# Loading w2 and w_out first, and forming their product while the other inputs arrive

## The chip, the cores and the metric

The kernel runs on one core of a Trainium2 chip. The metric is the device time of one execution in microseconds (us). Each time below is the median of several executions; the kernel before was run again on the same chip, in the same rounds, beside every experiment. A ratio is the mean time of one kernel's fast runs over that of the kernel before in the same rounds, with a 95% interval, so it isn't quite the ratio of the medians quoted. Profiles are of one execution each. A time "at 45.6" is counted from the start of that profile's span.

## The reference, cut to what matters

```python
k_proj = einsum('ks,bhsd->bhkd', E, k)          # 8 batches, 8 heads, 1024 tokens, 64 dims, 64 projected keys
v_proj = einsum('ks,bhsd->bhkd', F, v)
attn   = softmax(q @ k_proj.T / 8)
x      = attn @ v_proj                          # as 8192 tokens x 512
g      = maximum(x @ w1, x @ w2)                # w1, w2: 512 x 1024
out    = g @ w_out                              # w_out: 1024 x 512
```

The kernel uses maximum(h1, h2) = relu(h1 - h2) + h2. With wd = w1 - w2 and M = w2 @ w_out,

    out = relu(x @ wd) @ w_out + x @ M

so x goes through one wide product less, and M has to be formed once. Both products of later units are done with seven block products in place of eight, which takes sums and differences of blocks: those of w_out and M are called T, those of wd are t_w, those of g and x are "sums".

## The kernel before

All inputs are float32 in HBM and are cast to float16 on the way by DMAs issued from GpSimd. Batch 0's loads come first, then w2 and w1 in four pieces each, then w_out whole:

```python
for h0 in (0, H // 2):
    for n, src in (("k", k), ("q", q)):
        for h in (h0, h0 + H // 4):
            load(tiles[0], n, src, 0, h, h + H // 4)     # 256 KB of float16 each
    ...
load(tiles[0], "v", v, 0, 0, H // 2)
load(tiles[0], "v", v, 0, H // 2, H)
...
for f0 in range(0, DF, 256):
    for w_sb, w in ((w2_sb, moe_w2), (w1_sb, moe_w1)):
        nc.gpsimd.dma_start(out=w_sb[:, :, f0 : f0 + 256], in_=...)
nc.gpsimd.dma_start(out=wo_sb, in_=...)
```

Then come fillers, meant to keep TensorE's clock up (`warm(n)`: n matmuls of 128x512 whose result nobody reads), batch 0's attention, and its 16 up products (x @ wd), called slots. M is formed after the last of them, its transposes of w2 lying among them:

```python
def step_w2t(f0):                   # 8 transposes of w2, one copy on ScalarE
    ...
def step_m(r):                      # 8 matmuls of 128x512, one copy on ScalarE
    m_ps = mm_bank()
    for fb in range(NFB):
        nc.tensor.matmul(out=m_ps, lhsT=w2t_sb[:, fb, r * 128 : (r + 1) * 128],
                         rhs=wo_sb[:, fb, :], start=(fb == 0), stop=(fb == NFB - 1))
    nc.scalar.copy(out=m_sb[:, r, :], in_=m_ps)

slots = [ ... (2, u1[0]), (3, u1[1]), (4, u0[2]), (None, wt[0]), (5, u0[3]), ...
    *((16 + n, lambda n=n: step_m(n)) for n in range(NDC)) ]
for key, s_, *a in ( ...
    (15, sums_g, U[0, 0], (0, 1)), (16, step_t, 0), (16, sums_g, U[0, 0], (2, 3)),
    *((17 + i // 3, step_tw, i) for i in range(4)), (19, open_box, 3)):
    at_slot((0, key), s_, *a)       # VectorE's work beside slots 15 to 19
```

Batch 1's projection, its attention and the first down products follow ("batch 1's attention" below), then a steady pipeline to the end.

The softmax here doesn't subtract the row's maximum and nothing guards it: scores larger than these inputs give would overflow.

## Time and profile before

| | |
|---|---|
| time | 336.87 us (336.1 to 337.24, 3 runs) |
| span of the profiled run | 335.3 us |
| busy: PE, VectorE (DVE), ScalarE (ACT) | 325.3, 243.2, 225.3 us |
| DMA landings: first k, q pieces; v; w2 and w1; w_out | 8.2 to 17.3; 22.4; 23.7 to 33.1; 38.1 us |
| first projection of k / up products without a gap / M / batch 1's projection / batch 2's | 9.7 / 28.5 / 43.4 / 50.2 / 70.4 us |

In a timeline line the first two numbers are the start and the duration in us, then come engine, source line, operation, output<-inputs, shape and count, and in brackets how long the engine had idled and what ended it. The last row of the table is what the study follows: after batch 2's projection both kernels do the same, so its start tells the outcome.

### The profile page before, as it was taken

How to read it: one execution, taken by the hardware profiler on the slowest of the kernel's cores; microseconds unless marked ns; L12 is line 12 of the kernel's file. 1: busy time of each engine (PE TensorE's matmuls, PEld its weight loads, DVE VectorE, ACT ScalarE, POOL GpSimd, SP SyncE). 2: the span in 40 equal slices, each digit the busy share in tenths (PEclk: the TensorE clock that was granted, in tenths of full speed). 3: DMA queues.
4: the chain of work that ended last, by engine and by line, in shares of the span. 5: the costliest groups of instructions: out<-in, count | busy, mean ns of one | idle time of the engine just before them, and what ended most of it. 6: DMA issues, size and time to landing. Idle time of an engine off the chain costs nothing.

```text
span 335.3 us, 7334 instructions
## 1 busy us (share of the span) xinstructions
PE 325.3 (97%) x3020; PEld 245.9 (73%) x3020; DVE 243.2 (73%) x430; ACT 225.3 (67%) x354; POOL 34.4 (10%) x51
## 2 busy tenths in 40 slices
PE   6998999999999999999999999999999999999994
PEld 3544547578767887788878887888788888888883
DVE  1246898987776968787877967796878787868572
ACT  1287332955879787678778887878777877654541
POOL 7544002020003000200003000300000000000000
PEclk9799999999999999999999999999999999999998
DMA  7999999999886996699897999699742120202132
GB/s 136 204 201 199 207 207 207 218 232 187 174 190 82 208 226 158 118 178 243 184 164 110 225 179 200 113 211 231 183 95 94 33 97 31 96 31 96 34 125 94
DMA packets 71474, 51.98 MB, mean 155 GB/s; under 512 B 25233, under 2 KB 71313, under 8 KB 71441
## 3 DMA queue, kind: packets, MB, share of 16 engines
q0 software_dynamic: 30336, 28.31, 53.3%
q1 hardware_dynamic: 41104, 23.21, 27.7%
q8 instruction: 23, 0.38, 0.4%
q14 instruction: 11, 0.08, 0.1%
HBM read 57.15 MB, written 16.78 MB: 220 GB/s over the span
## 4 chain that ended last, share of the span: by engine, by line
PE 84%; DVE 8%; ACT 2%; DMA 2%; issue 1%; SPq 0%; DVEq 0%
PE mm_ps L699 39%; PE mm_ps L621 24%; PE mm_ps L467 4%; PE att_ps L180 3%; PE att_ps L365 3%; PE mm_ps L503 2%; PE mm_ps L280 2%; DMA big<-in_F_dram 2%; PE mm_ps L180 2%; DVE qt_sb L241 2%; PE mm_ps L139 1%; DVE xt_sb L446 1%; DVE o_sb L723 1%; DVE gt_sb L636 1%; DVE big L582 1%
## 5 line engine op out<-in xcount | busy, mean ns | idle before, releaser
L592 ACT COPY p_sb<-mm_ps 128x512 f32<-128x512 f32 x172 | 97.8, 597 | 38.0 <-PE mm_ps L621 23.5
L699 PEld LDWEIGHTS <-big 128*128 128x128 f16 x768 | 73.3, 98 | 14.6 <-issue 6.2
L699 PE MATMUL mm_ps<-T_sb,big 128*128 128x256 f16 x576 | 77.4, 273 | 0.0
L636 DVE TENSOR_TENSOR gt_sb<-mm_ps,p_sb 128x512 f16<-128x512 f32 x56 | 38.6, 689 | 48.4 <-PE mm_ps L621 26.7
L621 PE MATMUL mm_ps<-big,big 128*128 128x256 f16 x336 | 50.4, 272 | 0.2 <-DVE gt_sb L636 0.2
L621 PEld LDWEIGHTS <-big 128*128 128x128 f16 x448 | 43.8, 98 | 6.2 <-issue 0.4
L699 PEld LDWEIGHTS <-gt_sb 128*128 128x128 f16 x384 | 35.6, 98 | 12.3 <-issue 8.1
L699 PE MATMUL mm_ps<-wo_sb,gt_sb 128*128 128x256 f16 x256 | 42.7, 273 | 0.1
L621 PEld LDWEIGHTS <-wd_sb 128*128 128x128 f16 x336 | 32.9, 98 | 3.8
L621 PE MATMUL mm_ps<-xt_sb,wd_sb 128*128 128x256 f16 x224 | 33.6, 273 | 0.0
L381 DVE TENSOR_TENSOR xt_sb<-att_ps,ld_sb 128x1024 f16<-128x1024 f32 x24 | 29.3, 1222 | 1.8 <-ACT ld_sb L377 1.7
L723 DVE TENSOR_TENSOR o_sb<-mm_ps,p_sb 128x512 f32<-128x512 f32 x32 | 21.9, 685 | 9.4 <-PE mm_ps L699 5.9
L299 ACT ACTIVATE ex_sb<-mm_ps 128x512 f16<-128x512 f32 x40 | 21.8, 597 | 7.1 <-PE mm_ps L280 7.0
L377 ACT ACTIVATE ld_sb<-ld_sb 128x1024 f32<-128x1024 f32 x24 | 26.4, 1099 | 0.1
L374 ACT ACTIVATE ld_sb<-att_ps 128x1024 f32<-128x1024 f32 x24 | 24.8, 1035 | 0.6 <-PE att_ps L365 0.6
L699 PE MATMUL mm_ps<-m_sb,xt_sb 128*128 128x256 f16 x128 | 24.4, 273 | 0.0
L639 DVE TENSOR_SCALAR gt_sb<-gt_sb 128x512 f16<-128x512 f16 (+1 forms) x56 | 21.0, 374 | 1.9
L671 ACT ACTIVATE gt_sb<-mm_ps 128x512 f16<-128x512 f32 x28 | 16.8, 601 | 8.1 <-PE mm_ps L621 8.1
L582 DVE TENSOR_TENSOR big<-gt_sb 128x1024 f16<-128x1024 f16 x32 | 21.9, 685 | 0.3
L699 PE MATMUL mm_ps<-T_sb,gt_sb 128*128 128x256 f16 x128 | 21.5, 273 | 0.0
L699 PE MATMUL mm_ps<-wo_sb,big 128*128 128x256 f16 x128 | 21.5, 273 | 0.0
L699 PEld LDWEIGHTS <-xt_sb 128*128 128x128 f16 x192 | 18.8, 98 | 2.2
(106 smaller groups left out, 438.1 us busy)
## 6 DMA issues: line engine op xcount, KB each, us to landing
out_dram<-o_sb SPq DMA_DIRECT2D x63, 256.0 KB, 2.5
k_sb<-in_k_dram POOLq DMA_DIRECT2D x7, 1024.0 KB, 10.3
v_sb<-in_v_dram POOLq DMA_DIRECT2D x7, 1024.0 KB, 16.4
q_sb<-in_q_dram POOLq DMA_DIRECT2D x7, 1024.0 KB, 21.7
big<-in_moe_w_dram POOLq DMA_DIRECT2D x8, 256.0 KB, 12.6
k_sb<-in_k_dram POOLq DMA_DIRECT2D x4, 256.0 KB, 8.1
q_sb<-in_q_dram POOLq DMA_DIRECT2D x4, 256.0 KB, 9.2
v_sb<-in_v_dram POOLq DMA_DIRECT2D x2, 512.0 KB, 11.9
```

The source lines that it names most:

```text
L299: nc.scalar.activation(out=t["ex"][p][:, e, :], in_=banks[e], func=ACTF.Exp, scale=scale)
L374: nc.scalar.activation(out=ld, in_=dn_ps, func=ACTF.Ln)
L377: nc.scalar.activation(out=ld, in_=ld, func=ACTF.Exp, scale=-1.0)
L381: nc.vector.tensor_tensor(out=t["xt"][:, p, :, :], in0=at_ps, in1=ld, op=ALU.mult)
L582: nc.vector.tensor_tensor(out=S(i), in0=x, in1=y, op=op)
L592: copy(out=x, in_=bank)
L621: nc.tensor.matmul(out=bank[:, m * W : (m + 1) * W], lhsT=w_[:, n_, (2 * d + m) * 128 : (2 * d + m + 1) * 128], rhs=a[:, n_, :], start=(n ...
L636: nc.vector.tensor_tensor(out=c_blk(j, c), in0=two(x), in1=two(y), op=ALU.add)
L639: nc.vector.tensor_scalar_max(ap, ap, 0.0)
L671: nc.scalar.activation(out=out, in_=in_, func=ACTF.Relu)
L699: nc.tensor.matmul(out=bank[:, i * CH : (i + 1) * CH], lhsT=a(c)[:, i * 128 : (i + 1) * 128], rhs=w_(c), start=(n is not None and m == (lo ...
L723: nc.vector.tensor_tensor(out=o_sb, in0=two(x), in1=two(y), op=ALU.add)
```

## The change

The intent: PE waits for its first data until 9.7 us anyway. If w2 and w_out come first, M can be formed then, piece by piece as they land, and 8.7 us of PE work leave the middle.

```diff
+    for f0 in range(0, DF, 256):
+        fb = f0 // 128
+        load_w(w2_sb, moe_w2, f0, f0 + 256)
+        nc.gpsimd.dma_start(out=wo_sb[:, fb : fb + 2, :], in_=...[:, fb : fb + 2, :])
+        if f0 == 0:
+            make_identity(nc, ident)
     for h0 in (0, H // 2):
         ... loads of k and q ...
     load(tiles[0], "v", v, 0, 0, H // 2)
     load(tiles[0], "v", v, 0, H // 2, H)
     for f0 in range(0, DF, 256):
-        ... w2 and w1 ...
-    nc.gpsimd.dma_start(out=wo_sb, ...)
+        load_w(w1_sb, moe_w1, f0, f0 + 256)
     ...
+    m_ps = [mm_bank() for _ in range(NDC)]
+    def step_m(f0):                          # 8 matmuls: this piece's part of all four banks
+        for fb in (f0 // 128, f0 // 128 + 1):
+            for r in range(NDC):
+                nc.tensor.matmul(out=m_ps[r], lhsT=w2t_sb[:, fb, r * 128 : (r + 1) * 128],
+                    rhs=wo_sb[:, fb, :], start=(fb == 0), stop=(fb == NFB - 1), ...)
+    ... 6 fillers ...
+    step_w2t(0); step_m(0); step_w2t(256); step_eft(0); step_eft(1); step_m(256)
+    step_w2t(512); step_m(512); step_w2t(768); step_m(768)
+    for r in range(NDC):
+        eng = nc.vector.tensor_copy if r % 2 else nc.scalar.copy
+        eng(out=m_sb[:, r, :], in_=m_ps[r])
 ... batch 0's attention ...
+    step_t(0)                                # ahead of step_kv(t, 0, 4, "k")
     ...
+    step_t(1)                                # ahead of step_wd(0)
 ... up products: the four step_w2t taken out, slots 16 to 19 now empty ...
-        (15, sums_g, ...), (16, step_t, 0), (16, sums_g, ...), *((17 + i // 3, step_tw, i) ...),
+        (15, sums_g, ...), (15, sums_g, ...),
 ... batch 1's attention ...
-        if n in (1, 5):
-            at_slot(key, step_t, 1, (0, 1) if n == 1 else (2, 3))
+        if n in (2, 4, 7, 10):
+            at_slot(key, step_tw, (2, 4, 7, 10).index(n))
```

(The statements joined by semicolons are on lines of their own in the file, and `step_w2t`'s copy is halved between ScalarE and VectorE.)

More of the change, by code (lines that the diff above doesn't have):

```diff
@@ L109, with load_w @@
         alloc(tiles[0], n)
+    w1_sb = big(1).rearrange("p (r f) -> p r f", r=NDC)
+    w2_sb = big(2).rearrange("p (r f) -> p r f", r=NDC)
+    w2t_sb = big(3).rearrange("p (f m) -> p f m", f=NFB)
+    wo_sb = const.tile([128, NFB, DM], FP16)
+    def load_w(w_sb, w, f0, f1):
+        nc.gpsimd.dma_start(
+            out=w_sb[:, :, f0:f1], in_=w[:, f0:f1].rearrange("(r p) f -> p r f", p=128)
+        )
+    for f0 in range(0, DF, 256):
+        fb = f0 // 128
+        load_w(w2_sb, moe_w2, f0, f0 + 256)
+        nc.gpsimd.dma_start(
+            out=wo_sb[:, fb : fb + 2, :],
+            in_=moe_w_out.rearrange("(r p) f -> p r f", p=128)[:, fb : fb + 2, :],
+        )
+        if f0 == 0:
+            ident = const.tile([128, 128], FP32)
+            make_identity(nc, ident)
     for h0 in (0, H // 2):
@@ L113 @@
                 load(tiles[0], n, src, 0, h, h + H // 4)
-        if h0 == 0:
-            ident = const.tile([128, 128], FP32)
-            make_identity(nc, ident)
     load(tiles[0], "v", v, 0, 0, H // 2)
     load(tiles[0], "v", v, 0, H // 2, H)
-    w1_sb = big(1).rearrange("p (r f) -> p r f", r=NDC)
-    w2_sb = big(2).rearrange("p (r f) -> p r f", r=NDC)
-    wo_sb = const.tile([128, NFB, DM], FP16)
     for f0 in range(0, DF, 256):
-        for w_sb, w in ((w2_sb, moe_w2), (w1_sb, moe_w1)):
-            nc.gpsimd.dma_start(
-                out=w_sb[:, :, f0 : f0 + 256],
-                in_=w[:, f0 : f0 + 256].rearrange("(r p) f -> p r f", p=128),
-            )
-    nc.gpsimd.dma_start(out=wo_sb, in_=moe_w_out.rearrange("(r p) f -> p r f", p=128))
+        load_w(w1_sb, moe_w1, f0, f0 + 256)
     ones16 = const.tile([128, 512], FP16)
@@ L141, in warm, with step_eft @@
             )
-    warm(8)
     ident16 = const.tile([128, 128], FP16)
     nc.vector.tensor_copy(out=ident16, in_=ident)
+    m_sb = const.tile([128, NDC, DM], FP16)
     eft = const.tile([128, 2, NC, KP], FP16)
     ef_v = ef_sb.rearrange("kp i (p c) -> kp i c p", c=NC)
-    for i in range(2):
-        eft_ps = mm_bank()
+    def step_eft(i):
+        eft_ps = att_banks()[:, 0, :]
         for c in range(NC):
@@ L157, with step_w2t @@
             )
-        warm(2)
-        eng = nc.scalar.copy if i else nc.vector.tensor_copy
-        eng(out=eft[:, i, :, :].rearrange("p c k -> p (c k)"), in_=eft_ps)
+        nc.vector.tensor_copy(out=eft[:, i, :, :].rearrange("p c k -> p (c k)"), in_=eft_ps)
+    def step_w2t(f0):
+        ps_t = att_banks(FP16)[:, 0, :]
+        for f in range(2):
+            for r in range(NDC):
+                nc.tensor.transpose(
+                    out=ps_t[:, (f * NDC + r) * 128 : (f * NDC + r + 1) * 128],
+                    in_=w2_sb[:, r, f0 + f * 128 : f0 + (f + 1) * 128],
+                    identity=ident16,
+                )
+        for f, eng in enumerate((nc.scalar.copy, nc.vector.tensor_copy)):
+            eng(out=w2t_sb[:, f0 // 128 + f, :], in_=ps_t[:, f * DM : (f + 1) * DM])
+    m_ps = [mm_bank() for _ in range(NDC)]
+    def step_m(f0):
+        for fb in (f0 // 128, f0 // 128 + 1):
+            for r in range(NDC):
+                nc.tensor.matmul(
+                    out=m_ps[r], lhsT=w2t_sb[:, fb, r * 128 : (r + 1) * 128],
+                    rhs=wo_sb[:, fb, :],
+                    start=(fb == 0), stop=(fb == NFB - 1), skip_group_check=True,
+                )
+    w_ps = att_banks()[:, 0, :]
+    for _ in range(6):
+        nc.tensor.matmul(out=w_ps, lhsT=ones16[:, 0:128], rhs=ones16, start=True, stop=True)
+    step_w2t(0)
+    step_m(0)
+    step_w2t(256)
+    step_eft(0)
+    step_eft(1)
+    step_m(256)
+    step_w2t(512)
+    step_m(512)
+    step_w2t(768)
+    step_m(768)
+    for r in range(NDC):
+        eng = nc.vector.tensor_copy if r % 2 else nc.scalar.copy
+        eng(out=m_sb[:, r, :], in_=m_ps[r])
     def new_attn(t):
@@ L456 @@
     wd_sb = const.tile([128, NDC, DF], FP16)
-    m_sb = const.tile([128, NDC, DM], FP16)
-    w2t_sb = big(3).rearrange("p (f m) -> p f m", f=NFB)
     def up_slots(t, j):
@@ L484, in step_wd @@
         )
-    def step_w2t(f0):
-        ps_t = mm_bank(FP16)
-        for f in range(2):
-            for r in range(NDC):
-                nc.tensor.transpose(
-                    out=ps_t[:, (f * NDC + r) * 128 : (f * NDC + r + 1) * 128],
-                    in_=w2_sb[:, r, f0 + f * 128 : f0 + (f + 1) * 128],
-                    identity=ident16,
-                )
-        fb = f0 // 128
-        nc.scalar.copy(
-            out=w2t_sb[:, fb : fb + 2, :].rearrange("q f m -> q (f m)"), in_=ps_t
-        )
-    def step_m(r):
-        m_ps = mm_bank()
-        for fb in range(NFB):
-            nc.tensor.matmul(
-                out=m_ps, lhsT=w2t_sb[:, fb, r * 128 : (r + 1) * 128], rhs=wo_sb[:, fb, :],
-                start=(fb == 0), stop=(fb == NFB - 1),
-            )
-        nc.scalar.copy(out=m_sb[:, r, :], in_=m_ps)
     NG = NFB // 2
@@ L819 @@
     u0, u1 = [*up_slots(t, 0)], [*up_slots(t, 1)]
-    wt = [lambda f0=f0: step_w2t(f0) for f0 in range(0, DF, 256)]
     wd = [lambda f0=f0: step_wd(f0) for f0 in range(0, DF, 256)]
@@ L831 @@
         (0, u0[0]), (None, f(two_at, 1, 1)), (1, u0[1]), (None, lambda: loads(1, "v", "q", "k")),
-        (None, wd[1]), (2, u1[0]), (3, u1[1]), (4, u0[2]), (None, wt[0]), (5, u0[3]),
-        (None, wd[2]), (None, wt[1]), (6, u1[2]), (7, u1[3]), (8, u0[4]), (9, u0[5]), (None, wd[3]),
-        (None, wt[2]), (10, u1[4]), (11, u1[5]), (12, u0[6]), (13, u0[7]), (None, wt[3]),
+        (None, wd[1]), (2, u1[0]), (3, u1[1]), (4, u0[2]), (5, u0[3]),
+        (None, wd[2]), (6, u1[2]), (7, u1[3]), (8, u0[4]), (9, u0[5]), (None, wd[3]),
+        (10, u1[4]), (11, u1[5]), (12, u0[6]), (13, u0[7]),
         (14, u1[6]), (15, u1[7]),
-        *((16 + n, lambda n=n: step_m(n)) for n in range(NDC)),
+        *((16 + n, lambda: None) for n in range(4)),
     ]
@@ L870 @@
         (13, sums_x, U[0, 0], (1,)), (14, sums_x, U[0, 0], (3,)), (15, open_box, 0, 2),
-        (15, sums_g, U[0, 0], (0, 1)), (16, step_t, 0), (16, sums_g, U[0, 0], (2, 3)),
-        *((17 + i // 3, step_tw, i) for i in range(4)), (19, open_box, 3),
+        (15, sums_g, U[0, 0], (0, 1)), (15, sums_g, U[0, 0], (2, 3)), (19, open_box, 3),
     ):
```

## The prediction

> **What bounds the kernel now.** I read the page's slices first (40 slices of 8.4 us), then the timeline of the first 78 us, the only stretch the diff touches, then the DMA landings. From the slices:
>
> ```profile
> PE   6998999999999999999999999999999999999994
> DVE  1246898987776968787877967796878787868572
> PEclk9799999999999999999999999999999999999998
> DMA  7999999999886996699897999699742120202132
> ```
>
> PE is full from the fourth slice on, so past 78 us the kernel is bound by PE and any delay before it should come out at the end, unshortened. Only the first slices hold air. The DMA engines are full from slice 2 to 10: the loads form one queue that runs dry only around 58 us. Issue to landing, from the DMA view (the first line is that of the stretch 26.5 to 27.5 us, the others are the page's):
>
> ```profile
> v_sb<-in_v_dram POOLq DMA_DIRECT2D x1, 1024.0 KB, 21.3
> ...
> big<-in_moe_w_dram POOLq DMA_DIRECT2D x8, 256.0 KB, 12.6
> ...
> wo_sb<-in_moe_w_out_dram POOLq DMA_DIRECT2D x1, 1024.0 KB, 14.1
> ```
>
> Issue times plus these give landings: first k piece 8.2 us, then one 256 KB piece each 1.28 to 1.33 us (last k, q piece 17.3, v 22.4, first w1 piece 25.0, w_out 38.1), then batch 1's k 43.2, v 48.3, q 53.3. The timeline of the start:
>
> ```profile
> 1.46 3.59 PE L139 MATMUL mm_ps<-ones 128*128 128x512 f16 x8 [1.46 <-DVE ones L132]
> ...
> 9.71 1.88 PE L180 MATMUL mm_ps<-k_sb,eft 128*64 128x256 f16 x8
> ...
> 11.64 0.42 DVE L190 CAST kp_sb<-mm_ps 64x256 f16<-64x256 f32 x1 [4.83 <-PE mm_ps L180]
> ...
> 15.06 1.94 ACT L406 ACTIVATE ex_sb<-att_ps 128x1024 f16<-128x1024 f32 x2 [5.58 <-PE att_ps L398]
> ...
> 25.25 0.68 DVE L481 TENSOR_TENSOR wd_sb<-big,big 128x1024 f16<-128x1024 f16 x1
> ...
> 25.93 1.29 DVE L446 TENSOR_TENSOR xt_sb<-mm_ps,rec_sb 128x512 f16<-128x512 f32 x2
> ...
> 28.46 3.61 PE L467 MATMUL mm_ps<-xt_sb,wd_sb 128*128 128x512 f16 x16 [0.19 <-DVE xt_sb L446]
> ...
> 31.91 0.61 PE L490 MATMUL mm_ps<-ident,big 128*128 128x128 f16 x8
> ...
> 32.61 1.01 ACT L496 COPY big<-mm_ps 128x1024 f16<-128x1024 f16 x1
> ```
>
> Batch 0's attention starts when its first k has landed (9.6, start 9.71). From there each load is in before its use (k 14.7 for 16.05, q 17.3 for 19.04, v 19.8 for 21.59): the stretch from 9.71 to 28.46 is a chain PE to DVE to ACT, not a wait for data. Then come 16 up products, with four groups of w2 transposes among them, and M:
>
> ```profile
> 43.20 7.07 PE L503 MATMUL mm_ps<-wo_sb,big 128*128 128x512 f16 x32
> ...
> 45.60 0.68 DVE L538 TENSOR_TENSOR T_sb<-wo_sb 128x1024 f16<-128x1024 f16 x1
> ...
> 49.33 0.69 DVE L538 TENSOR_TENSOR big<-wd_sb 128x1024 f16<-128x1024 f16 x1
> ...
> 50.20 0.40 PE L180 MATMUL mm_ps<-k_sb,eft 128*64 128x512 f16 x1
> ...
> 54.28 0.43 DVE L538 TENSOR_TENSOR T_sb<-m_sb 128x512 f16<-128x512 f16 x1
> ```
>
> While PE does M, VectorE does twelve subtractions (sums of g, T, and those of wd) that nobody waits for. M is a shelter for them.
>
> **What the Trainium skill says.** "DMA: Bandwidth & Descriptors", Measured: large loads issued from GpSimd reach 425 GB/s. Here a piece of 256 KB (512 KB of float32 in HBM) takes 1.31 us, about 400 GB/s read: agrees, so order decides who waits and no order makes the queue shorter. "TensorE: Matmul & The Clock Gate", Part 1: the array runs at half rate until about 3.4 us of activity, and drops back after an idle window. The trace agrees: the eight first matmuls took 3.59 us (0.43 each, against 0.216 later), and the granted clock is 0.50 between 10 and 12 us. "PSUM — Partial Sum Buffer", Engine vs sequencer instructions: ScalarE and VectorE queues are strict FIFO and matmuls complete in program order. Agrees: no order in the trace departs from the program's. "VectorE: DVE Perf Modes", The TRN2 errata: a fixed term of about 150 cycles measured on a copy; with two elements a cycle that gives (512 + 150) / 0.96 = 690 ns for a 128x1024 float16 subtraction; the trace has 681 to 692.
>
> **The change part by part.**
>
> *Removed from the middle.* Four groups of transposes at 0.45 us (the chain's figure) are 1.8 us; M is 6.9 us (43.36 to 50.27). PE gets 8.7 us back before batch 1's projection. This is the whole gain.
>
> *Put at the start: when does M end?* The first weight piece lands where the first k piece did, 8.2, and w_out's last, eighth, at 17.3. PE's order is fixed: transposes, M part, and so on.
> - Transposes of piece 0 at 8.3. Six warm-up matmuls end near 4.0, so PE was idle for 4.2 us, and I take it cold: 0.85 us, copies 0.6 plus 0.3 of hand-overs. M part 0 at 10.1: eight matmuls at 0.43 until the clock comes back near 12.4 (as before), done 13.0.
> - Transposes of piece 1, 0.45: 13.45. Both E, F transposes, 1.09 each as before: 15.65. M part 1, 8 x 0.216 = 1.73: 17.4.
> - From here each piece is serial, since its M part follows its own transposes: transposes 0.6, copy 0.6, hand-overs 0.3 to 0.4, matmuls 1.73: 3.3. Twice: 24.0.
>
> So M ends at 24.0, estimated, 6.7 after its data; warm throughout it would be 22.5, with another cold window 26.
>
> *Attention's new start.* Its first k is in (19.9) but its PE work follows M. VectorE: two copies of m (to M + 0.9), then the four subtractions of T from w_out (2.55 from start to start in the old trace), so kp's copy starts at M + 3.5 to 3.6, where k's own matmuls ended at M + 1.1. So about 2.5 us of formerly sheltered subtractions lie on the path. From kp's copy to the first exp took 3.42 with cold warm-ups in it, 3.1 without: exp at M + 6.7 = 30.7, before 15.06. Delay 15.6.
>
> *From exp to the continuous up products.* 28.46 - 15.06 = 13.4. VectorE is without a gap from 23.7 to 29.7, and the other four subtractions of T (from m, 0.4 each) are put there ahead of wd: + 1.6. Up products from 30.7 + 15.0 = 45.7. w1 lands 34 to 38 and v by 32.7, estimates at 1.3 a piece: no wait.
>
> *Up products.* 15 x 4 x 0.216 = 13.0, taken as 13.2, as VectorE is tight in the last eight (eight evictions of 0.69, four sums of 0.42, one wd of 0.68 = 7.9 us against PE's 6.9). They end at 58.9, and batch 1's projection follows at once: 50.2 before, so + 8.7.
>
> *Batch 1's attention beside the first down products.* The sums of g (four, 2.6) come after the last eviction and are no longer sheltered, so batch 1's v copies start about 1.1 later after their matmuls. In this stretch VectorE loses 4 x 0.43 and gets 4 x 0.69: + 1.0. It was busy for 3.92, 3.75, 3.63 and 3.00 of four windows of 4 us (54 to 70), so about 1.7 is absorbed. I take + 0.8.
>
> Sum: delay of attention 15.6 + 1.6 + shorter up stretch (13.2 - 14.9 = - 1.7) - 6.9 (M) + 0.1 (rounding) + 0.8 = 9.5. 336.87 + 9.5 = 346.4.
>
> **The rivals.**
> - *M fills idle time and the DMA queue binds next.* For it: PE does nothing useful before 9.7. Then batch 1's projection moves up to its v's landing, 48.3, which is 1.9 earlier, and q's transposes only from 54.4 to 53.3: about 335.5. Against: k stands behind eight weight pieces, some 10.3 us, more than the 8.7 that M costs.
> - *PE keeps up with the landings.* M ends at 17.3 + 1.8, attention starts at 19.9 instead of 9.7 and pays T: 10.2 - 8.7 + 2.5 + 1.6 + 0.8 - 0.8 (k's matmuls now at full clock) = 5.6: 342.5. Against: the copies stand between transposes and M in each piece, and the cold window falls on M part 0.
> - *The subtractions cost nothing*, as VectorE waits anyway. Then 9.5 - 4.1 = 5.4: 342.3. Against: its queue is in order and has no gap in the old trace after 23.7.
> - *The clock stays low for another window*, because E, F transposes fill few rows of the array: + 2: 348.5. For it: the window that held them, 5.6 to 9.0, was followed by the half clock.
>
> **Range and chances.** M's end (22.5 to 26) and how much of T hides make plus or minus 3 each way; both weaker variants give some 342.4, the cold one 348.5. Range 341.5 to 349.5. The threshold of 2% is 343.6. Most of my mass is above; two of the errors together bring it below. Faster by 2% would be 330.1, below anything the DMA queue allows here. Faster 0.01, same 0.22, slower 0.77.
>
> **What would show it.** Right: M's last matmul at 22.5 to 26, no wait for DMA there; T between m's copies and kp's copy on VectorE, with PE waiting for kp; first exp near 30.7; up products from 45.7; batch 1's projection near 58.9 with its v long landed; everything after shifted by a constant. Wrong: M done by 20 and k waiting for its DMA; kp copied without T before it; batch 1's projection waiting for v at 48.3; or the later stretch giving time back.

## The result, and the profile after

The changed kernel takes 346.87 us (345.68 to 348.08, 4 runs) against 336.75 us before (4 runs): ratio 1.0291 (1.0254 to 1.0328), slower by 2.9%. The results are correct. The four runs lie at two levels, 345.7 and 345.8, and 347.9 and 348.1; the profiled one is of the upper level.

The slices of the changed kernel, to be laid beside those in the prediction:

```profile
PE   4978799999999999999999999999999999999994
DVE  0243659999687796779677868877877968677672
PEclk9998989999999999999999999999999999999999
DMA  9999996699969599959984999699871212122032
```

Among the first six slices four of PE are under 9 in place of two, and there are two dips of the granted clock (fourth and sixth slice) in place of one. In these six slices DMA is as full as before: the change reorders the loads and doesn't shorten them. (Its dip to 6 in slices seven and eight, where it was 9, comes later: batch 2's loads of v and q were issued at 62.2 and 63.1 in place of 52.4 and 53.3, after the later projection of batch 1.) The timeline of the changed kernel:

```profile
7.00 1.03 PE L173 MATMUL att_ps<-ident,big 128*128 128x128 f16 x8 [2.80 <-DMA big<-in_moe_w_dram]
...
8.71 3.60 PE L186 MATMUL mm_ps<-wo_sb,big 128*128 128x512 f16 x8 [0.68 <-ACT big L179]
...
21.37 1.90 PE L186 MATMUL mm_ps<-wo_sb,big 128*128 128x512 f16 x8 [0.68 <-ACT big L179]
...
23.30 1.03 PE L227 MATMUL mm_ps<-k_sb,eft 128*64 128x256 f16 x8
24.08 0.68 DVE L554 TENSOR_TENSOR T_sb<-wo_sb 128x1024 f16<-128x1024 f16 x1
...
26.61 0.41 DVE L237 CAST kp_sb<-mm_ps 64x256 f16<-64x256 f32 x1
27.07 0.31 PE L257 MATMUL mm_ps<-ident,kp_sb 64*64 64x64 f16 x8 [2.21 <-DVE kp_sb L237]
...
31.00 1.94 ACT L453 ACTIVATE ex_sb<-att_ps 128x1024 f16<-128x1024 f32 x2 [7.27 <-PE att_ps L445]
...
41.04 0.42 DVE L554 TENSOR_TENSOR T_sb<-m_sb 128x512 f16<-128x512 f16 x1
...
42.50 0.68 DVE L526 TENSOR_TENSOR wd_sb<-big,big 128x1024 f16<-128x1024 f16 x1
...
45.63 14.46 PE L512 MATMUL mm_ps<-xt_sb,wd_sb 128*128 128x512 f16 x60
```

M's last part ends at 23.3, where its last data landed at 16.3. The half clock of M's start (the clock's record begins at 14.27), the E and F transposes and the copies between transposes and M parts (0.68 idle before each) took the rest. k's own matmuls begin at 23.30 without a wait for data, as k had landed at 18.9: 4.4 us earlier. Then VectorE makes T before it copies kp, and PE sits idle for 2.21 us. The first exp is at 31.00, where it was at 15.06.

The windows view of the changed kernel (start and end, length, then the busy time of PE, weight loads, VectorE, ScalarE and GpSimd with instruction counts, then granted clock, DMA share, GB/s), cut along the clock's own stretches:

```profile
24.51:27.92 3.41, 1.20 (x15) 0.57 (x14) 2.77 (x6) 0.00 (x0) 1.40 (x2) 1.00 1.24 206
27.92:31.33 3.41, 3.41 (x36) 2.13 (x33) 1.39 (x2) 0.33 (x1) 0.00 (x0) 0.50 1.28 203
41.57:44.98 3.41, 1.37 (x17) 0.40 (x6) 3.41 (x8) 2.18 (x3) 0.20 (x1) 1.00 1.24 207
44.98:48.40 3.42, 3.42 (x16) 1.26 (x16) 2.49 (x5) 1.19 (x2) 0.00 (x0) 0.50 1.24 207
```

Each time VectorE makes T (first and third line), PE is busy for 35 to 40% of 3.4 us, and in the next 3.4 us it is granted half its clock. This is why q's transposes took 1.76 us instead of 1.06 and the 60 up matmuls 14.4 us, where 60 x 0.216 = 13.0 would do.

Where it ends, in the chain of the kernel before and then of the changed one (start, length, what), the last line of each being batch 1's projection:

```profile
43.36 6.91 PE mm_ps L503 x32
50.27 1.89 PE mm_ps L180 x16
```

```profile
45.67 14.42 PE mm_ps L512 x60
60.09 1.85 PE mm_ps L227 x16
```

The projection is at 60.0 instead of 50.2 (9.8 later), batch 2's at 80.9 instead of 70.4 (10.5 later), and the span 10.9 us longer in this profile. Nothing is given back later.

### The profile page after: what moved, and what is told of

It reads as the page before. It is cut to its first block, busy times and chain, and to the rows that moved or that the text cites. A ratio compares the mean times of both kernels' runs of the same rounds, so it can differ in the third digit from the quotient of the medians.

```text
span 346.2 us, 7330 instructions
## 1 busy us (share of the span) xinstructions
PE 328.3 (95%) x3014; PEld 247.2 (71%) x3014; DVE 245.8 (71%) x437; ACT 222.1 (64%) x351; POOL 36.6 (11%) x54
## 4 chain that ended last, share of the span: by engine, by line
PE 83%; DVE 9%; ACT 2%; issue 2%; DMA 2%; DVEq 0%; POOLq 0%
PE mm_ps L715 39%; PE mm_ps L637 23%; PE mm_ps L512 5%; PE att_ps L227 3%; PE att_ps L412 3%; PE mm_ps L186 3%; PE mm_ps L327 2%; DMA big<-in_moe_w_dram 2%; DVE qt_sb L288 1%; DVE gt_sb L652 1%; PE mm_ps L227 1%; DVE xt_sb L428 1%; PE mm_ps L147 1%; DVE T_sb L554 1%; DVE o_sb L739 1%
## 6 DMA issues: line engine op xcount, KB each, us to landing
q_sb<-in_q_dram POOLq DMA_DIRECT2D x4, 256.0 KB, 10.1
```

## The experiments

The theory, called A: the load order alone pushes batch 0's attention back by about as much as M costs, so the early M can at best break even; and in leaving the middle, M uncovers VectorE's subtractions, which then lie on the path and let PE's clock halve. The rivals: that the early M's own slowness on PE is all of the loss; that VectorE would have waited anyway; that the idea wins once its flaws are mended; and, for the kernel before, that M's PE time counts in full.

| run | edit | time, us | ratio to before (95%) | batch 1's projection at |
|---|---|---|---|---|
| before | | 336.75 | | 50.2 |
| changed | | 346.87 | 1.0291 (1.0254 to 1.0328) | 60.0 |
| e1 | changed, T among the up products | 341.95 | 1.0156 (1.0113 to 1.0199) | 54.1 |
| e2 | changed, fillers in PE's gaps | 343.28 | 1.0186 (1.0157 to 1.0215) | 54.4 |
| e3 | before, loads in the new order | 347.66 | 1.0307 (1.0281 to 1.0333) | 60.8 |
| e4 | before, M nearly left out (wrong) | 336.46 | 0.9980 (0.9949 to 1.0012) | 44.7, stalls to 47.6 |
| e5 | changed, T moved and start reordered | 340.30 | 1.0094 (1.0073 to 1.0114) | 53.7 |
| e6 | e5, and work moved to ScalarE | 339.57 | 1.0065 (1.0041 to 1.0088) | 51.7 |
| e7 | before, one copy on ScalarE | 336.76 | 0.9996 (0.9978 to 1.0013) | 50.7 |
| e8 | before, five more fillers | 336.09 | 0.9983 (0.9962 to 1.0004) | 49.0 |
| e9 | e6, start without fillers in the way | 337.27 | 1.0008 (0.9987 to 1.0030) | 50.8 |
| e10 | e8 once more | 336.82 | 0.9993 (0.9969 to 1.0017) | 49.2 |

### e1: T moved to where VectorE is idle

```diff
-    step_t(0)                     # ahead of batch 0's k
-    step_t(1)                     # ahead of step_wd(0)
+        (2, step_t, 0, (0, 1)), (3, step_t, 0, (2, 3)),        # beside up slots 2 to 6
+        (4, step_t, 1, (0, 1)), (5, step_t, 1, (2,)), (6, step_t, 1, (3,)),
```

> The changed kernel with the eight subtractions that make T moved out of batch 0's attention into the up products, where VectorE was idle (0.51 us busy between 48 and 52 us). Theory A (the subtractions lie on the path to the first exp and to the up products, and the idle PE time that they make brings the half clock back twice): kp's copy comes some 2.6 us earlier, the up products start at about 40.5 instead of 45.6 and some of the half clock goes; 340.5 to 342.5 us. Theory B (VectorE would have waited anyway; only the later start behind the weights counts): 346 to 347 us. Theory C (the loss moves into batch 1's attention, where VectorE is full): 344 to 346 us.

Measured: 341.95 us, 4.9 below the changed kernel. The timeline of e1:

```profile
23.95 0.41 DVE L237 CAST kp_sb<-mm_ps 64x256 f16<-64x256 f32 x1 [0.20 <-PE mm_ps L227]
...
26.99 1.94 ACT L453 ACTIVATE ex_sb<-att_ps 128x1024 f16<-128x1024 f32 x2 [3.67 <-PE att_ps L445]
...
42.12 0.68 DVE L554 TENSOR_TENSOR T_sb<-wo_sb 128x1024 f16<-128x1024 f16 x1
```

kp's copy follows k's matmuls (which began at 22.88) at once, the first exp is 4.0 earlier than in the changed kernel, and the granted clock stays at 1.00 from 13.1 us on. The time lies inside what theory A expected, and both rivals fall. So about half of the loss came from where T stood: from its own 4.1 us, and from the two dips of the clock that followed it.

### e2: fillers where PE is idle

```diff
-    for _ in range(6):            # fillers at the start
+    for _ in range(12):
     step_kv(t, 0, 4, "k")
-    warm(2)
+    warm(12)
     two_at(t, 0, 1)
+    ... 8 fillers ...             # ahead of the first up product
```

> The changed kernel with more warm-up matmuls in PE's idle time (12 instead of 6 at the start, 12 instead of 2 while kp is waited for, 8 ahead of the first up product) and nothing else. Theory A (the stretches at half clock, 28 to 31 and 44 to 48 us and M's first part, cost time of their own): no granted clock under 0.9 after 10 us, M done about 1.5 us earlier, the up products as a block 1.2 us shorter, in all 3 to 4 us less: 343 to 344 us. Theory B (the clock only fills time that is idle anyway): 346.5 to 347.5 us.

Measured: 343.28 us, 3.6 below the changed kernel. In e2 the clock is at 1.00 from 5.0 us on, k's projection starts at 20.3 instead of 23.3, and

```profile
41.37 13.11 PE L512 MATMUL mm_ps<-xt_sb,wd_sb 128*128 128x512 f16 x60 [0.19 <-DVE xt_sb L493]
```

takes 13.1 us, not 14.5. T is still on the path here; no work was removed, only matmuls that nobody reads were added. So the clock has a price of its own beside T's. The profile has k's projection 3.0 us earlier (0.5 of it from an earlier first landing), and some 1.35 us less each from there to the first exp and in the up products. e1 and e2 overlap in these two dips, so their gains (4.9 and 3.6) can't be added.

### e3: the new load order alone

The loads are the changed kernel's; all computing stays where the kernel before has it.

```diff
+    ... w2 and w_out in four pieces each, then k, q, v, then w1, as in the changed kernel ...
-    ... k, q, v, then w2 and w1, then w_out ...
```

> The kernel before with the loads in the changed order and its computing left where it was. Theory A (eight weight pieces ahead of k push attention back by their 9.2 us, 18.9 instead of 9.7, and nothing gives that back): first projection at 18.9, M at about 52.5, batch 1's projection at about 59.4, 345.5 to 346.5 us, so the changed kernel's early M buys nothing at all on top of its load order. Theory B (the early M itself is what costs, since PE ran behind the landings): 337 to 340 us here.

Measured: 347.66 us, ratio 1.0307, 1.2 above the top of theory A's range and not to be told from the changed kernel. In the timeline of e3:

```profile
19.10 1.89 PE L188 MATMUL mm_ps<-k_sb,eft 128*64 128x256 f16 x8 [11.06 <-DMA k_sb<-in_k_dram]
...
39.06 3.61 PE L475 MATMUL mm_ps<-xt_sb,wd_sb 128*128 128x512 f16 x16 [0.19 <-DVE xt_sb L454]
...
60.80 0.40 PE L188 MATMUL mm_ps<-k_sb,eft 128*64 128x512 f16 x1
```

PE idles 11.06 us for k, and the clock is at half from 11.5 to 25.1, which I hadn't counted. Against the kernel before, k's projection starts 9.4 us later (19.10, not 9.71), the up products 10.6 (39.06, not 28.46), and batch 1's projection 10.6: 9.4 from the order, and 1.2 more within batch 0's attention, where the clock was low.

That the order alone costs as much as the whole change is the main finding: the changed kernel takes 8.7 us of PE work from the middle of e3 and ends where e3 ends. The starts in the two profiles say what took it. In the changed kernel k's projection is 4.2 us later than in e3 (23.30, not 19.10), as M runs past k's landing; from there to the first exp takes 0.9 longer, and from exp to the up products 1.5. From the up products to batch 1's projection takes 7.4 less: M's 8.7, short of what the clock's dip cost. The largest item is M's own late end; e2 gets 3.0 of it back, mostly by the clock. e3 also shelters half of T (the four subtractions from w_out) under M, as the kernel before does; the other four lie in batch 1's attention there.

### e4: M nearly left out of the kernel before

```diff
-        for fb in range(NFB):                 # step_m: 1 of 8 matmuls for each bank
+        for fb in range(1):
-    wt = [lambda f0=f0: step_w2t(f0) ...]     # 1 of 4 groups of transposes
+    wt = [lambda f0=f0: step_w2t(f0) if f0 == 0 else None ...]
```

Its output is wrong, which doesn't matter for the time.

> The kernel before, wrong on purpose: 4 of M's 32 matmuls and one of four groups of w2 transposes, so some 7.4 us of PE work leaves the middle without anything being put anywhere. Theory A (M is a shelter: VectorE's twelve subtractions and the landing of batch 1's v at 48.3 us and q at 53.3 take its place): batch 1's projection no earlier than 48.3, time 334.5 to 337 us, so at most 2 us of 7.4 come through. Theory B (PE is the bound and its work counts in full): 329 to 330.5 us.

Measured: 336.46 us, ratio 0.9980 (0.9949 to 1.0012): of 7.4 us removed, some 0.7 comes through, by the interval at most 1.7. In the timeline of e4, around batch 1's projection:

```profile
44.67 0.38 PE L180 MATMUL mm_ps<-k_sb,eft 128*64 128x512 f16 x1 [0.85 <-ACT m_sb L507]
...
47.56 0.58 PE L180 MATMUL mm_ps<-v_sb,eft 128*64 128x512 f16 x1 [2.52 <-DMA v_sb<-in_v_dram]
```

PE is there at 44.67, then waits for batch 1's v, which landed at 47.5, and runs the projection at half clock (0.63 for a matmul that takes 0.38). With this load order the stage couldn't start more than some 2 to 3 us earlier (47.56, not 50.2) even if M cost nothing anywhere, since v's landing sets it. So the gain that the change was after wasn't there to be had in the kernel before.

### e5, e6 and e9: the early M at its best

e5 keeps e1's edit, moves the E and F transposes ahead of the first weight piece, and takes transposes ahead of the M part before them:

```diff
+    fill(6); step_eft(0); fill(3); step_eft(1); fill(2)
     step_w2t(0)
+    fill(4)
     step_m(0)
     step_w2t(256)
-    step_eft(0); step_eft(1)
+    fill(4)
     step_m(256)
     step_w2t(512)
-    step_m(512)
     step_w2t(768)
+    step_m(512)
     step_m(768)
```

> The early M at its best: T's subtractions among the up products as in e1, the E and F transposes moved ahead of the first weight piece, transposes of later pieces ahead of the M part before them so that their copies are hidden, fillers in PE's gaps. Theory A (what is left is the landing of k behind eight weight pieces, 18.9 us, against 8.7 us of PE work taken from the middle): M done by about 19.0, first projection of k between 18.9 and 19.5, up products from about 36, batch 1's projection at 49.5 to 50.5, where the kernel before has it at 50.2, and batch 1's attention some 1 to 1.5 us longer; 336.5 to 338.5 us, no win. Theory B (the idea wins once its flaws are mended): 331 to 334 us.

Measured: 340.30 us, above both ranges. k's projection began at 22.4, not at 19. The timeline of e5 shows why:

```profile
9.11 1.01 PE L173 MATMUL att_ps<-ident,big 128*128 128x128 f16 x8
...
11.62 2.97 PE L186 MATMUL mm_ps<-wo_sb,big 128*128 128x512 f16 x8
```

The first w2 piece had landed at 6.5, and its transposes ran at 9.1: my fillers and the E and F transposes, at half clock by their durations (three fillers took 1.46 us), stood in the way. A miss of the experiment's design, and it left open whether the idea could win.

e6 adds to e5:

```diff
-                if fb < 3:                    # evictions of up products on ScalarE, the others on VectorE
+                if fb < 5:
-            st["s1"] = keep_d(...)            # first kept product of batch 0's first unit: VectorE
+            st["s1"] = keep("pd", ...)        # ScalarE
```

> e5 with two more of eight evictions of each up group and the first kept product of batch 0's first unit moved from VectorE to ScalarE, which is idle there. Theory A (the longer attention of batch 1 comes from VectorE's queue): 0.7 to 1.5 us below e5, so 335.5 to 337.5, about level with the kernel before or just below it. Theory B (it comes from PE or from loads): same as e5 within 0.4.

Measured: 339.57 us, 0.7 below e5, at the lower end of what theory A expected; the absolute range was missed since e5's was. The two ratios' intervals overlap, and e6's profiled run began k at 21.1 where e5's began at 22.4 with the same code ahead of it, so the times alone don't show that the moved work helped. The length of one stretch does: batch 1's attention, from projection to projection, is 20.2 us long as in the kernel before, where it is 20.9 in the changed kernel, e1 and e5.

e9 takes e6's start apart once more:

```diff
     step_eft(0)
-    fill(3)
     step_eft(1)
-    fill(2)
     step_w2t(0)
-    fill(4)
     step_m(0)
     step_w2t(256)
-    fill(4)
+    step_w2t(512)
     step_m(256)
-    step_w2t(512)
     step_w2t(768)
```

> e6 without the fillers at the start, which held up the first w2 transposes (9.1 us in e5, landed at 6.5), and with the transposes of piece 2 ahead of M part 1. Theory A (k's landing is the floor, at some 18.7 us; e5 and e6 started k at 22.4 and 21.1): M done at 19 to 20, k's projection at 19 to 20.5, batch 1's projection at 49.8 to 51, time 336 to 338.5 us, level with the kernel before. Theory B (the start is still PE at half clock): k's projection stays at 21 or later and the time at e6's 339.6.

Measured: 337.27 us against 336.87, ratio 1.0008 (0.9987 to 1.0030). In e9, k's second piece landed at 19.5 and

```profile
20.18 1.03 PE L230 MATMUL mm_ps<-k_sb,eft 128*64 128x256 f16 x8
...
37.69 13.21 PE L515 MATMUL mm_ps<-xt_sb,wd_sb 128*128 128x512 f16 x60 [0.19 <-DVE xt_sb L496]
...
50.82 0.40 PE L230 MATMUL mm_ps<-k_sb,eft 128*64 128x512 f16 x1
```

so the start is within 0.7 us of its data. T is off the path, the clock's later dips are gone, and batch 1's attention is 20.2 us long. With all that mended, the early M is level with the kernel before and not better: 10.5 us later for k (20.2 against 9.7) against 8.7 us less of PE work in the middle, with attention running 1.2 us faster (17.5 from k to the up products, 18.7 before) as the clock doesn't halve in it. 10.5 - 8.7 - 1.2 = 0.6, which is by how much batch 1's projection is later (50.8 against 50.2). It ends where theory A put it. e9 also has e6's evictions on ScalarE, which the kernel before was not given, so level is a generous reading for the early M.

### e7, e8 and e10: the kernel before, two controls

e7 moves one copy to ScalarE, as in e6; e8 adds fillers at the start; e10 is e8 again.

```diff
-            st["s1"] = keep_d(...)            # e7
+            st["s1"] = keep("pd", ...)
-        warm(2)                               # e8, e10: after the E and the F transposes
+        warm(3 if i else 6)
```

> The kernel before with only the first kept product of batch 0's first unit copied by ScalarE instead of VectorE. A control for e6: if VectorE's queue sets the pace of batch 1's attention, 0.4 to 0.8 us faster than before (ratio 0.998); if not, 1.000.

Measured: 336.76 us, ratio 0.9996. In the kernel before this copy isn't worth anything, so e6's shorter attention of batch 1 is more likely due to the evictions than to this copy; e6 didn't separate the two.

> The kernel before with 5 more fillers between the E and F transposes, so that the granted clock does not halve at 9 us. Theory A (the start of the kernel before is just in time with its loads: w1's first piece lands at 25.0 and wd begins at 25.25, batch 1's q lands at 53.3 and is used at 54.4): the first projection is 0.8 us shorter and at most 0.3 us of it arrives, ratio 0.998 to 1.001. Theory B (PE's start sets the end): 0.8 to 1.5 us faster, ratio 0.996.

> e8 once more, as its interval (0.9962 to 1.0004) still holds 1. If keeping the clock up between 9 and 12 us is worth its 1.2 us, the ratio is 0.996 to 0.998 with runs at clock 1.0 near 336 and runs at 0.992 near 337.3; if e8 was chance, 0.999 to 1.000.

Measured: 336.09 and 336.82 us, ratios 0.9983 and 0.9993, both intervals holding 1. The twelve runs lie at two levels: seven at a mean clock of 1.000 take 335.8 to 336.3 us, five at 0.991 or 0.992 take 337.2 to 337.6. So about 1.2 us lie between a run with a dip of the clock and one without, but that these fillers bring the lower level isn't shown: the kernel before had runs at 336.0 to 336.1 too (one with a mean clock of 0.992), and one of 337.2 at 1.000. Nor is 9 to 12 us the only place for a dip: e7's profiled run, of 337.46 us and without these fillers, kept the full clock there and had the half clock from 26.4 to 29.8. The landings differ as well. My reason for expecting next to nothing, that loads are just in time, was only partly right: in e8's profile, a run of the lower level, they landed 0.9 to 1.8 us earlier than in the profile of before (first k piece at 6.4, not 8.2), so the limit moved with them. No version was found that clearly beats the kernel before.

## Why the prediction was right

The predicted 346.4 us met 346.87, and the steps held with these sizes. Times are starts in the profiles.

| step | predicted | measured |
|---|---|---|
| first weight piece lands | 8.2 | 7.0 |
| M ends | 24.0 | 23.3 |
| kp's copy after M's end | 3.5 to 3.6 | 3.3 |
| first exp | 30.7 | 31.0 |
| up products without a gap | 45.7 | 45.6 |
| length of their block | 13.2 | 14.4 |
| batch 1's projection | 58.9 | 60.0 |
| batch 1's attention, longer by | 0.8 | 0.7 |
| delay in all | 9.5 | 10.1 (medians), 10.9 (profiles) |

*M's end* came out nearly right by errors that offset each other. The work began 1.3 us earlier, at 7.0 (first landings lay between 6.3 and 8.2 us over the runs of either order), and the later pieces took 0.4 less. But the half clock, which I had end near 12.4, within M's first part, held for all of that part (eight matmuls in 3.60 us, from 8.71) and the transposes after it (1.06 us): 1.0 more. The clock's own record starts only at 14.3 in this profile, so before that the durations tell it, and the windows view's 1.00 there is no measurement.

*T on the path* was right and was the step most open to doubt: e1 removes it and gains 4.9 us, where I had 4.1 for T.

*The clock* is what I left out. I took it to matter only while M is formed, and named a further cold window as a rival for that stage alone. The runs show two more, at 27.9 and 45.0, both after a stretch in which PE waited for VectorE's T. They cost 1.3 us between kp and the first exp (4.39 us from kp's copy, 3.04 in e1) and 1.2 in the up products' block. That the sum still fits is partly luck: M was 0.7 early, and the stretch from exp to the up products 0.4 shorter than I had. e2's earlier k shows that the half clock while M is formed was the dearest of the three.

*The rivals.* That PE would keep up with the landings was wrong: M ended 7.0 us after its last data (16.3 and 23.3), not 1.8. That batch 1's projection would come to wait for its v is wrong for the change, as it comes 12 us after v, but e4 shows that this is the limit when M's time goes without the load order: it was my ground for giving a gain of 2% almost no chance, and it holds.

*Loose readings.* In the prediction's slices PE's fourth is an 8, so PE isn't full there. The queue doesn't run dry at 58 us either: between 58 and 70 the view's DMA share is 1.21 to 1.25, as before 58. Neither enters the sum. The prediction takes the half clock at 10 to 12 us for a drop after an idle window, but PE was busy for 2.26 of the 3.41 us before it. That transposes which fill few rows of the array hold the clock down was a guess that no run here tests. The 690 ns for a subtraction is an estimate from the page's figures; the sum used the trace's starts.

*The gain that was expected.* e3 and e4 settle where the 8.7 us of PE time went. The load order costs all of what the change costs (1.0307 for it alone, 1.0291 with the early M), and the time saved in the middle is worth next to nothing by itself in the kernel before (0.9980 with M nearly gone), since batch 1's v landed between 47.4 and 48.3 in all the profiles, of either order. In the changed kernel the load order has moved the middle back so far that v no longer binds; there the 8.7 us count, but M's late end (4.2 us after e3's start of k), T, the clock's dips and the unsheltered sums take them. e9, with these mended, gets them and comes out level.

What stays open: the two levels of the changed kernel's runs (2.3 us apart). Their mean granted clocks don't tell them apart (0.988 and 0.989 above, 0.988 twice below), and only a run of the upper level was profiled. No other load order was tried, such as k's first pieces ahead of the weights, nor were e6's evictions tried in the kernel before.

## What to carry to other kernels

When loads form one queue that is full up to a later stage, ask of each load that is moved ahead what it pushes back, and look first at where that later stage's own data lands: no work removed before it can bring it closer than that. Work of the bounding engine may shelter another engine's work; before moving it, list what runs beside it, and find that a new shelter (e1: 4.9 us). An idle stretch on TensorE can cost twice: after the gaps of 2.0, 2.2 and 2.5 us shown here (changed kernel and e4) the clock was halved for some 3.4 us.

## What the Trainium skill lacked or had wrong

- "TensorE: Matmul & The Clock Gate", Part 1 and its rule for authors, has the clock halve after an idle window of about 3.4 us and asks for no idle gap over 3 us. Here one gap of 2.2 us and one of 2.0 us, in windows in which PE was busy for 1.20 and 1.37 of 3.41 us, were each followed by 3.4 us at 0.50. A gap well under 3 us can be enough.
- The same page puts the ramp's penalty at under 1% of a typical kernel and advises against fitting a count of cold matmuls. Here fillers alone (e2, which also fill two later gaps) gained 3.6 us of 346.9. At 1.0% the size is near the page's, but it is a third of the 10.1 us at issue, so it had to be modelled.
- The same page doesn't give the busy time that suffices. PE was busy for 2.26 of 3.41 us before the half clock of the kernel before (with float32 transposes of 64 rows in it), and for 2.22 of 3.41 us in e2, after which the clock stayed full: busy time in the trace doesn't decide it. The page's Part 4 does say that transposes don't count as busy in the same way. Both of these windows hold transposes, and no run here tells how much theirs count.
- "DMA: Bandwidth & Descriptors", Measured, gives the time of a DMA by size and advises 1 MB or more, and the page's section on queues tells how descriptors are taken and warns that DMAs need not complete in order. Neither gives what a piece takes behind others. Here pieces of 512 KB read, issued from GpSimd, landed in the order of their issue, one each 1.2 to 1.5 us, near 400 GB/s; the bytes ahead of a piece set its landing (w_out's last piece 16.3, k's second 18.9).
